# Tile 0 of x in two half loads on two queues, x 3 ahead of Q's second weight block, Q 0 and Q 1 in turn, and fewer idle matmuls, in a fused linear attention and SwiGLU kernel

## The chip, the cores and the metric

The kernel runs on one core of one Trainium2 chip. The metric is the device time of one execution in microseconds (us). The engines of the core are TensorE (PE in the profile, with its weight loads as PEld), VectorE (DVE), ScalarE (ACT), GpSimd (POOL) and SyncE (SP). Here only SP and ACT issue loads and stores; what they issue is shown as SPq and ACTq, and the transfers themselves are done by 16 DMA engines.

## The reference

The input x is 2048 rows of 512 bf16 numbers. The output is x plus two branches of the same layer-normed x.

```python
x = A_x                                             # (1, 2048, 512)
xn = (x - mean) / sqrt(var + 1e-5)                  # over the last axis
# branch A: linear attention, 32 heads of 16
q, k, v = split(xn @ wqkv)                          # wqkv (512, 1536)
phi = lambda t: where(t > 0, t + 1, exp(t)) + 1e-6
pq, pk = phi(q), phi(k)
num = pq @ (pk^T v) ; den = pq . sum_s(pk) + 1e-6   # per head
A = concat(num / den) @ wo
# branch B: SwiGLU, inner width 1792
B = (silu(xn @ w_gate) * (xn @ w_up)) @ w_down
return x + A + B
```

## The kernel before

The rows of x are cut into 16 tiles of 128 rows, held in `x_sb`. Tile t goes through mean and variance (`bns`, `agg`: DVE's bn_stats and bn_aggr), normalisation, a transpose, the projections to K and Q (four matmuls each, one for each block of 128 input columns: blocks 0 to 3 of the weights "wk" and "wq"), the feature map, and an accumulation (`gtacc`, L590) of xn^T times the K features. Only after all 16 tiles come the large products of the SwiGLU branch (L785) and the output products (L979, L990).

The first four tiles take a shorter way. They are only centred (`xc_half`, `xc_full`: x minus mean), transposed and projected, and the factor 1/std (`rstd`) is put in where ACT reads the result. For tiles 0 to 2 the transpose is done on TensorE (`tp_first`, L410, two matmuls against `ident` for each half) with a copy by ACT (`tc_first`, L422); for tile 3 it is a DMA transpose on SP's queue (`transpose_xc`, L401). The mean of tile 1 comes from ACT (`mean_act`, L307), not from DVE. `proj_part` (L465) is one projection matmul with one block; `proj_first` (L452) is two.

The order of the work is written out by hand. The program calls helpers in one list; each helper appends to the list of its engine, and each engine runs its list in order. Dependencies are kept by name: an operation waits for the last writer of each name it reads, and for the readers of each name it writes. Each DMA has its own semaphore. Two consequences matter here. The load of x 1 on ACT's queue reads the name ("ident",), so that it waits for POOL's memset of `ident`, and the affine_select (L242) that completes `ident` waits in turn for that load to land. And the transposes wait for `ident`.

Before x 0 is there, TensorE runs idle matmuls on constants: `fill(n, cols)` issues n matmuls of `cols` columns into bank 3 (L271). There are eight of 512 columns ahead of the first transpose, and one of 128 between the two halves of tile 0.

The loads are issued in this order. SP: x 0, K's blocks 0 and 1 in one load, K's block 2, x 2, Q's blocks 0 and 1, x 3, Q's blocks 2 and 3, x 4, x 5, x 6 with x 7. ACT: x 1, K's block 3. In K's projection TensorE takes the blocks in the order 0, 1, 3, 2; in Q's projection the order was blocks 0 and 1 of tile 1, blocks 0 and 1 of tile 0, the transposes of tile 2, and then blocks 2 and 3 in turn for the two tiles.

Of the kernel before, what the change touches and what calls it, by code (L numbers as in the profile page):

```python
# [10 lines left out]
P = 128  # L11
# [98 lines left out]
def bass_parallel_sum__linear_attn_block__swiglu_ffn__prompt_kernel(  # L110
# [10 lines left out]
    xin = A_x[0]  # L121
    oview = out[0]
    K = _Prog()
    pe, act, dve, pool, sp = nc.tensor, nc.scalar, nc.vector, nc.gpsimd, nc.sync
    bf, f32 = dt.bfloat16, dt.float32

    with contextlib.ExitStack() as es:
        E = es.enter_context

        def sb(name, shape, d=bf):  # L130
            return E(nc.sbuf_tensor(name, [P] + shape, d))

        x_sb = sb("x_sb", [NT, D])
# [14 lines left out]
        stats = sb("stats", [NT, 6], f32)  # L148
# [43 lines left out]
        def bk(i):  # L192
            return ("bank", i)
# [5 lines left out]
        def rows(v, t0, n):  # L199
            if t0 < NLONE:  # L200
                return v[t0 * P:(t0 + n) * P, :].rearrange("(t p) d -> p t d", p=P)
            return v[NLONE * P:, :].rearrange("(p t) d -> p t d", t=NT - NLONE)[:, t0 - NLONE:t0 - NLONE + n, :]

        def xload(eng, h, t0, n, after=()):
            K.dma(
                eng, lambda: h.dma_start(x_sb[:, t0:t0 + n, :], rows(xin, t0, n)),
                r=list(after), w=[("x", t0 + i) for i in range(n)],
            )

        def wqkv_load(eng, h, name, i, c0, n, after=()):  # L210
            K.dma(
                eng,
                lambda: h.dma_start(
                    wqkv_sb[:, c0:c0 + n, i * D:(i + 1) * D],
                    A_wqkv[c0 * P:(c0 + n) * P, i * D:(i + 1) * D].rearrange("(c p) f -> p c f", p=P),
                ),
                r=list(after), w=[(name, c) for c in range(c0, c0 + n)],
            )
# [6 lines left out]
        def whalf(name, dst, src, h):  # L225
# [6 lines left out]
                w=[(name, h)],  # L232
            )

        K.op("pool", lambda: pool.memset(warm[:, :], 0.0), w=[("warm",)])
        K.op("act", lambda: act.activation(warm[:, :], warm[:, :], ACT.Exp), r=[("warm",)], w=[("warm",)])

# [8 lines left out]
            r=[("ident",)], w=[("ident",)],  # L246
        )
        K.op("pool", lambda: pool.memset(nhalf[:, :], -0.5), w=[("nhalf",)])

        xload("sp", sp, 0, 1)  # L250
        wqkv_load("sp", sp, "wk", 1, 0, 2)
        wqkv_load("act", act, "wk", 1, 3, 1)
        wqkv_load("sp", sp, "wk", 1, 2, 1)
        xload("sp", sp, 2, 1)
        wqkv_load("sp", sp, "wq", 0, 0, 1)
        wqkv_load("sp", sp, "wq", 0, 1, 1)
        xload("sp", sp, 3, 1)
        wqkv_load("sp", sp, "wq", 0, 2, 1)
        wqkv_load("sp", sp, "wq", 0, 3, 1)
        xload("sp", sp, 4, 1)  # L260
# [6 lines left out]
        def fill(n, cols, after=()):  # L267
            K.op(
                "pe",
                [  # L270
                    (lambda: pe.matmul(banks[3][:, 0:cols], cw, cx[:, 0:cols], start=True, stop=True))  # L271
                    for _ in range(n)
                ],
                r=list(after), w=[bk(3)],
            )
# [20 lines left out]


        def bns(t):
            K.op("dve", lambda: dve.bn_stats(stats[:, t, :], x_sb[:, t, :]), r=[("x", t)], w=[("st", t)])  # L299

        def agg(t):
            K.op("dve", lambda: dve.bn_aggr(mv[:, t, :], stats[:, t, :]), r=[("st", t)], w=[("mv", t)])
# [95 lines left out]
        def transpose_xc(t):  # L398
            K.dma(
                "sp",  # L400
                lambda: sp.dma_start_transpose(out=xcT[:, NDC * t:NDC * (t + 1), :], in_=xc_sb[:, t, :]),  # L401
                r=[("xc", t, 0), ("xc", t, 1)], w=[("xcT", t, 0), ("xcT", t, 1)],
            )
# [57 lines left out]
        def proj_part(t, wname, c, pos):  # L461
            lo, b = (D, kb(t)) if wname == "wk" else (0, qb(t))
            K.op(
                "pe",
                lambda: pe.matmul(  # L465
                    banks[b], xcT[:, NDC * t + c, :], wqkv_sb[:, c, lo:lo + D],
                    start=(pos == 0), stop=(pos == NDC - 1),
                ),
                r=[("xcT", t, c // 2), (wname, c)], w=[bk(b)],
            )  # L470

        def kb(t):
            return 2 * (t % 2)

        def qb(t):
            return 2 * (t % 2) + 1
# [122 lines left out]
        def stat(t):  # L599
            bns(t)  # L600
            agg(t)
            eps(t, "pool")
            rstd_of(t)
# [3 lines left out]
            if t >= 3:  # L607
                transpose_dma(t)

        fill(8, 512)  # L610
        bns(0)
        agg(0)
        xc_half(0, 0)
# [10 lines left out]
        tp_first(1, 0, 6)  # L624
        tc_first(1, 0, 6)
        bns(1)
        rstd_of(0)
        xn_dve(0)
# [19 lines left out]
        proj_part(1, "wk", 3, 2)  # L648
        proj_part(1, "wk", 2, 3)
        proj_part(1, "wq", 0, 0)  # L650
        proj_part(1, "wq", 1, 1)
        transpose_xc(3)
        xload("sp", sp, 8, 2)
        xload("sp", sp, 10, 2)
        proj_part(0, "wq", 0, 0)
        proj_part(0, "wq", 1, 1)
        first_pk(0)
        tp_first(2, 0, 4)
# [429 lines left out]
```

## Time and profile before

| | |
|---|---|
| time, median of 3 runs | 210.25 us (210.12 to 210.37) |
| time of the profiled execution | 210.51 us |
| its span, first to last instruction | 209.3 us, so 1.2 us lie around it |
| TensorE busy | 206.6 us, 99% of the span |
| DVE, ACT, POOL busy | 120.2, 70.9, 72.0 us |
| DMA moved | 16.84 MB, mean 80 GB/s |

Rows of the timeline read: start in us, duration in us, engine, source line, operation, output tile <- input tiles, shape, count, and in brackets the idle time before it and what ended it. Where a count is over one, the duration runs from the start of the first to the end of the last. A matmul's duration includes its drain, so that matmuls in a row overlap; the spacing of their starts is what each costs. A row with an arrow from a tensor in DRAM and a number at its end is a load with its median time from issue to landing. Rows that begin with a stretch A:B give the length, the busy time of PE, PEld, DVE, ACT and POOL (with counts), the granted clock, the DMA share and GB/s.

### The profile page before, as it was taken

Reading aid. Unit: us, or ns where it says so; the run is one execution under the profiler, and the core shown is the slowest. Engines: PE = TensorE matmul, PEld = TensorE weight load, DVE = VectorE, ACT = ScalarE, POOL = GpSimd, SP = SyncE. Lnnn points to the kernel's source line nnn. Section 1 sums busy time; section 2 is a strip of 40 time slices with the busy share of each in tenths; the row PEclk is TensorE's granted clock in tenths of the full one; section 3 lists DMA queues with packets and bytes.
Section 4 is the critical chain, followed back from the end, with each engine's and each line's share of the span. In section 5 each row is a group of like instructions: output and inputs, shape, how many; then the busy total and the mean of one; then the engine's idle time right before and its main releaser. Section 6 shows DMA issues by size and latency. Waiting matters only on the chain.

```text
span 209.3 us, 2824 instructions
## 1 busy us (share of the span) xinstructions
PE 206.6 (99%) x1015; PEld 94.6 (45%) x1015; DVE 120.2 (57%) x246; ACT 70.9 (34%) x125; POOL 72.0 (34%) x90
## 2 busy tenths in 40 slices
PE   8999999999999999999999999999999999999996
PEld 3444444444444444444444444444444444444444
DVE  3999988336365874637355746365556545374122
ACT  5777666966643331312112312213031213121000
POOL 3427977568032543223041422240424132221200
PEclk9999999999999999999999999999999999999999
DMA  6673644894797011010101110102011010110101
GB/s 200 209 195 75 127 100 100 256 364 158 202 357 50 11 39 25 28 25 25 50 2 50 28 29 22 50 0 53 6 45 25 27 28 25 49 30 25 50 28 50
DMA packets 30287, 16.84 MB, mean 80 GB/s; under 512 B 20928, under 2 KB 29632, under 8 KB 30272
## 3 DMA queue, kind: packets, MB, share of 16 engines
q1 hardware_dynamic: 29984, 16.39, 29.9%
q10 hardware_dynamic: 288, 0.26, 0.4%
q8 instruction: 8, 0.13, 0.2%
q14 instruction: 7, 0.06, 0.1%
HBM read 9.70 MB, written 2.10 MB: 56 GB/s over the span
## 4 chain that ended last, share of the span: by engine, by line
PE 99%; DVE 0%; issue 0%
PE psum L785 46%; PE psum L990 23%; PE psum L438 10%; PE psum L979 7%; PE psum L590 7%; PE psum L271 2%; PE psum L465 2%; PE psum L452 2%; PE psum L410 1%; PE psum L892 0%; PE psum L915 0%; DVE out_sb L1003 0%
## 5 line engine op out<-in xcount | busy, mean ns | idle before, releaser
L800 ACT ACTIVATE sg<-psum 128x512 bf16<-128x512 f32 x56 | 33.4, 598 | 106.0 <-PE psum L785 102.5
L785 PE MATMUL psum<-xnT,wg_sb 128*128 128x512 bf16 x224 | 57.5, 379 | 0.0
L785 PE MATMUL psum<-xnT,wu_sb 128*128 128x512 bf16 x224 | 57.5, 379 | 0.0
L934 POOL TENSOR_TENSOR prod<-pkq,zb 128x512 f32<-128x512 bf16 x16 | 18.6, 1163 | 55.9 <-DVE pkq L514 55.9
L785 PEld LDWEIGHTS psum<-xnT,wu_sb 128*128 128x128 bf16 x224 | 21.9, 98 | 26.4
L785 PEld LDWEIGHTS psum<-xnT,wg_sb 128*128 128x128 bf16 x224 | 21.8, 98 | 26.2 <-issue 0.2
L1003 DVE TENSOR_TENSOR out_sb<-psum,x_sb 128x512 bf16<-128x512 f32 (+2 forms) x17 | 11.2, 660 | 35.9 <-PE psum L990 35.9
L958 POOL TENSOR_TENSOR pqn<-pkq,rden 128x512 bf16<-128x512 bf16 x16 | 16.9, 1056 | 36.5 <-DVE rden L952 36.5
L806 DVE TENSOR_TENSOR pkq<-psum,sg 128x512 bf16<-128x512 f32 x28 | 19.2, 686 | 17.1 <-PE psum L785 14.7
L806 DVE TENSOR_TENSOR xn_sb<-psum,sg 128x512 bf16<-128x512 f32 x28 | 18.8, 673 | 14.1 <-PE psum L785 13.6
L990 PE MATMUL psum<-wd_sb,xn_sb 128*128 128x512 bf16 (+2 forms) x126 | 25.7, 355 | 0.0
L990 PE MATMUL psum<-wd_sb,pkq 128*128 128x512 bf16 x112 | 25.5, 379 | 0.0
L438 PE MATMUL psum<-wqkv_sb,xnT 128*128 128x512 bf16 x96 | 22.5, 379 | 0.0
L582 POOL TENSOR_TENSOR zacc<-zacc,pkq 128x512 f32<-128x512 f32 x15 | 17.3, 1155 | 5.0 <-DVE ek L505 4.6
L990 PEld LDWEIGHTS psum<-wd_sb,xn_sb 128*128 128x128 bf16 x126 | 11.8, 98 | 12.5
L990 PEld LDWEIGHTS psum<-wd_sb,pkq 128*128 128x128 bf16 x112 | 11.0, 98 | 13.2
L979 PE MATMUL psum<-m_sb,eq 128*128 128x512 bf16 (+2 forms) x68 | 16.6, 366 | 0.0
L590 PE MATMUL psum<-pkq,xn_sb 128*128 128x512 bf16 x64 | 15.9, 379 | 0.0
L438 PEld LDWEIGHTS psum<-wqkv_sb,xnT 128*128 128x128 bf16 x96 | 9.4, 98 | 11.3
L942 DVE TENSOR_REDUCE den<-prod 128x32 f32<-128x512 f32 x16 | 10.9, 683 | 5.9 <-POOL prod L934 5.9
L299 DVE BATCH_NORM_STATS2 stats<-x_sb 128x6 f32<-128x512 bf16 x16 | 10.9, 681 | 3.4 <-DMA x_sb<-in_A_x_dram 3.4
L514 DVE SCALAR_TENSOR_TENSOR pkq<-pkq,eq 128x512 bf16<-128x512 bf16 x16 | 11.1, 692 | 0.6
(68 smaller groups left out, 138.7 us busy)
## 6 DMA issues: line engine op xcount, KB each, us to landing
out_dram<-out_sb SPq DMA_DIRECT2D x15, 128.0 KB, 1.7
wg_sb<-in_B_w_gate_dram SPq DMA_DIRECT2D x2, 896.0 KB, 7.8
wu_sb<-in_B_w_up_dram SPq DMA_DIRECT2D x2, 896.0 KB, 6.1
wd_sb<-in_B_w_down_dram SPq DMA_DIRECT2D x1, 1792.0 KB, 11.1
x_sb<-in_A_x_dram SPq DMA_DIRECT2D x5, 256.0 KB, 3.1
x_sb<-in_A_x_dram SPq DMA_DIRECT2D x5, 128.0 KB, 3.4
wqkv_sb<-in_A_wqkv_dram SPq DMA_DIRECT2D x5, 128.0 KB, 3.8
wqkv_sb<-in_A_wqkv_dram SPq DMA_DIRECT2D x1, 512.0 KB, 7.9
```

Of the source, the lines that this page charges most:

```text
L438: (lambda c=c: pe.matmul(banks[b], xnT[:, c, t * P:(t + 1) * P], wqkv_sb[:, c, lo:lo + D], start=(c == 0), stop=(c == NDC - 1),))
L514: lambda: dve.scalar_tensor_tensor(out=dst, in0=src, scalar=0.0, in1=e, op0=ALU.max, op1=ALU.add,),
L582: lambda: pool.tensor_tensor(out=zacc[:, :], in0=zacc[:, :], in1=pk, op=ALU.add),
L590: (lambda c=c: pe.matmul(banks[4 + c], xn_sb[:, t, c * P:(c + 1) * P], pkq[:, t, 0, :], start=(t == 0), stop=(t == NT - 1),))
L785: (lambda c=c: pe.matmul(banks[b], w_sb[:, c, fc * P:(fc + 1) * P], xnT[:, c, C * 512:(C + 1) * 512], start=(c == 0), stop=(c == NDC - 1),))
L800: lambda: act.activation(sg[:, j % NSG, :], banks[gb], ACT.Silu),
L806: lambda: dve.tensor_tensor(out=hT(C, fc), in0=banks[ub], in1=sg[:, j % NSG, :], op=ALU.mult,),
L934: lambda: pool.tensor_tensor(out=p, in0=pkq[:, t, 1, :], in1=zb[:, :], op=ALU.mult),
L958: lambda: pool.tensor_tensor(out=pqn[:, t % NPN, :].rearrange("p (i g h e) -> p g i h e", i=NB, g=NG, e=DH), in0=pkq[:, t, 1, :].rearrange ...
L979: (lambda g=g: pe.matmul(dst, pqnT(t)[:, g, :], m_sb[:, g, lo:hi], start=(g == 0), stop=False,))
L990: (lambda fc=fc: pe.matmul(dst, hT(C, fc)[:, jj * P:(jj + 1) * P], wd_sb[:, fc, lo:hi], start=False, stop=(fc == NFC - 1),))
L1003: lambda: dve.tensor_tensor(out=o, in0=src, in1=x_sb[:, t, lo:hi], op=ALU.add),
```

## The change

x 0 is loaded by two DMAs of 64 rows each, one as SP's first load and one as ACT's first load, ahead of all else on those engines. The second has a name of its own, ("xb", 0), and `bns` reads it too. On SP, x 3 is issued one place earlier, ahead of Q's block 1. The eight idle matmuls of 512 columns become seven of 512 and one of 128. In the list of projections, block 0 of Q is done for tile 1 and tile 0, then block 1 for tile 1 and tile 0; the issue of tile 3's DMA transpose and of two loads of x stands between them.

```diff
+        def xhalf(eng, h, t, lo, name):
+            K.dma(
+                eng, lambda: h.dma_start(x_sb[lo:lo + P // 2, t, :], rows(xin, t, 1)[lo:lo + P // 2, 0, :]),
+                w=[(name, t)],
+            )
+
+        xhalf("sp", sp, 0, 0, "x")
+        xhalf("act", act, 0, P // 2, "xb")
         K.op("pool", lambda: pool.memset(warm[:, :], 0.0), w=[("warm",)])
         K.op("act", lambda: act.activation(warm[:, :], warm[:, :], ACT.Exp), r=[("warm",)], w=[("warm",)])
...
-        xload("sp", sp, 0, 1)
         wqkv_load("sp", sp, "wk", 1, 0, 2)
         wqkv_load("act", act, "wk", 1, 3, 1)
         wqkv_load("sp", sp, "wk", 1, 2, 1)
         xload("sp", sp, 2, 1)
         wqkv_load("sp", sp, "wq", 0, 0, 1)
+        xload("sp", sp, 3, 1)
         wqkv_load("sp", sp, "wq", 0, 1, 1)
-        xload("sp", sp, 3, 1)
         wqkv_load("sp", sp, "wq", 0, 2, 1)
...
         def bns(t):
-            K.op("dve", lambda: dve.bn_stats(stats[:, t, :], x_sb[:, t, :]), r=[("x", t)], w=[("st", t)])
+            K.op("dve", lambda: dve.bn_stats(stats[:, t, :], x_sb[:, t, :]), r=[("x", t), ("xb", t)], w=[("st", t)])
...
-        fill(8, 512)
+        fill(7, 512)
+        fill(1, P)
         bns(0)
...
         proj_part(1, "wq", 0, 0)
-        proj_part(1, "wq", 1, 1)
+        proj_part(0, "wq", 0, 0)
         transpose_xc(3)
         xload("sp", sp, 8, 2)
         xload("sp", sp, 10, 2)
-        proj_part(0, "wq", 0, 0)
+        proj_part(1, "wq", 1, 1)
         proj_part(0, "wq", 1, 1)
```

## The prediction

> **What bounds the kernel now.** I read the page first (busy shares, slices, chain), then the chain of waits in order of time, then the timeline of the first 12 us, then the landings of single loads.
>
> ```profile
> PE 206.6 (99%) x1015; PEld 94.6 (45%) x1015; DVE 120.2 (57%) x246; ACT 70.9 (34%) x125; POOL 72.0 (34%) x90
> PE   8999999999999999999999999999999999999996
> PE 99%; DVE 0%; issue 0%
> ...
> 0.84 3.57 PE psum L271 x8
> 4.41 0.36 PE psum L410 x2
> ```
>
> TensorE is busy for 99% of the span and is the chain from 0.84 us to the end. Nothing the diff touches lies later than the first 12 us, so the question is only how much earlier or later TensorE's stream leaves its opening. The opening starts with eight idle matmuls (L271) and goes on with the transposes of tile 0 (L410). The busy row hides two holes there, because a matmul's shown duration covers its drain; the weight loads (PEld) show them.
>
> ```profile
> 2.93 0.15 PEld L271 LDWEIGHTS psum<-const-bfloat16-1.0 128*128 128x128 bf16 x1 [0.28 <-issue]
> 3.35 0.15 PEld L271 LDWEIGHTS psum<-const-bfloat16-1.0 128*128 128x128 bf16 x1 [0.28 <-issue]
> 3.08 0.69 DVE L299 BATCH_NORM_STATS2 stats<-x_sb 128x6 f32<-128x512 bf16 x1 [3.08 <-DMA x_sb<-in_A_x_dram]
> 3.81 0.18 DVE L302 BATCH_NORM_AGGREGATE mv<-stats 128x2 f32<-128x6 f32 x1
> 4.03 0.48 DVE L382 TENSOR_SCALAR xc_sb<-x_sb,mv 128x256 bf16<-128x256 bf16 x2
> 4.37 0.13 PEld L410 LDWEIGHTS psum<-ident,xc_sb 128*128 128x128 bf16 x2 [0.87 <-DVE xc_sb L382]
> ```
>
> Idle matmuls follow each other every 0.42 us (2.93, 3.35). The last loads at 3.35 + 0.42 = 3.77 and has streamed by about 4.2; the first transpose starts at 4.37, released by DVE's centred tile, which goes back to tile 0's landing (bn_stats at 3.08). So the bound of the opening is not the idle matmuls but the chain x 0, statistics, centring; the idle matmuls end 0.17 ahead of it.
>
> ```profile
> 5.31 0.66 PE L465 MATMUL psum<-wqkv_sb,xcT 128*128 128x512 bf16 x2
> 5.91 0.10 PEld L465 LDWEIGHTS psum<-wqkv_sb,xcT 128*128 128x128 bf16 x1 [0.45 <-ACT xcT L422]
> 4.80 1.25 ACT L422 ACTIVATE xcT<-psum 128x256 bf16<-128x256 bf16 x4 [0.71 <-PE psum L410]
> 8.32 1.03 PE L465 MATMUL psum<-wqkv_sb,xcT 128*128 128x512 bf16 x4
> ```
>
> Second hole: K's first two blocks for tile 0 start at 5.31 and 5.31 + 0.66 - 0.38 = 5.59, the third, block 3, has its weights loaded only at 5.91. The page names ACT's copy, but of the four copies from 4.80 to 6.05 the second, which is the one needed, had ended near 5.5. The other input of that matmul is K's block 3 of weights, loaded on ACT's queue.
>
> ```profile
> 1.48 0.45 ACTq L213 DMA_DIRECT2D wqkv_sb<-in_A_wqkv_dram  x1
> wqkv_sb<-in_A_wqkv_dram ACTq DMA_DIRECT2D x1, 128.0 KB, 4.3
> ```
>
> Issued at 1.48 and 4.3 us to landing: 5.78, which is what the weight load at 5.91 waited for. The four matmuls of the row at 8.32 (1.03 for four, 0.38 each with its drain) give a spacing of (1.03 - 0.38) / 3 = 0.217 at full clock against 0.42 at the start. Between 5.31 and 5.59 lies a mixture: 0.28 = part at 0.42, rest at 0.217, which puts the change of clock near 5.44. After 5.91 TensorE runs at 0.217 without a hole.
>
> **The loads.** ACT gets a new first load.
>
> ```profile
> 0.80 0.39 SPq L206 DMA_DIRECT2D x_sb<-in_A_x_dram  x1
> 0.80 1.28 ACT L236 ACT_TABLE_LOAD   x1 [0.80 <-PEq L1073]
> 1.07 0.38 ACTq L206 DMA_DIRECT2D x_sb<-in_A_x_dram  x1
> 1.25 0.93 SPq L213 DMA_DIRECT2D wqkv_sb<-in_A_wqkv_dram  x2
> 3.37 0.63 ACT L307 ACTIVATE scr<-x_sb 128x512 bf16<-128x512 bf16 x1 [1.08 <-DMA x_sb<-in_A_x_dram]
> 1.80:2.20 0.40, 0.40 (x3) 0.13 (x1) 0.00 (x0) 0.39 (x2) 0.00 (x0) 1.00 0.47 151
> 2.20:2.70 0.50, 0.50 (x3) 0.17 (x2) 0.00 (x0) 0.09 (x1) 0.00 (x0) 1.00 1.07 373
> ```
>
> From issue to first use x 0 takes 3.08 - 0.80 = 2.28 us on SP and x 1 takes 3.37 - 1.07 = 2.30 on ACT. In the first 0.4 us of traffic only SP's rows flow, at 151 GB/s (last number); with both queues in flight it is 373. If one queue's rate is what limits x 0, its first 60 KB (0.4 x 151) came in that stretch and the other 68 KB shared 373 with x 1, done about 68 / 187 = 0.36 later, at 2.56; two queues at twice 151 would have brought all 128 KB by about 2.22. So the split is worth between 0.34 us and nothing, or minus 0.05 for a second semaphore that bn_stats now waits for and ACT's own 0.02 of delay. I take the middle, 0.17. Here the Trainium skill (DMA: Bandwidth & Descriptors, Rules for kernel authors) speaks against the change: two transfers to disjoint partition halves spray over the same 16 engines, so one 128-partition transfer is advised. By it the gain is zero; the 151 against 373 in this trace says that the engines are not yet full when x 0 arrives, and there the two differ.
>
> With 0.17: transposes start at 4.37 - 0.17 = 4.20. The idle matmuls, 384 columns shorter (0.75 x 0.42 = 0.32), stop near 3.89 instead of 4.2. That cut alone gains nothing: 0.17 was idle already, and what waits is DVE's chain. If x 0 gains nothing, TensorE simply idles 0.48 instead of 0.17. What it avoids is that an idle matmul runs past 4.20.
>
> The price stands on ACT's queue. The table load ran beside the x 1 load (0.80 for 1.28, and 1.07), so it does not hold the issue; but xb at 0.80 takes a slot, and loads on a queue follow each other at 0.41 (ACT, 1.07 to 1.48) to 0.45 (SP, 0.80 to 1.25). So x 1 is issued at about 1.25 and K's block 3 at 1.66, each 0.18 later.
>
> ```profile
> 3.57 0.29 POOL L242 TENSOR_SCALAR_AFFINE_SELECT ident<-ident 128x128 bf16<-128x128 bf16 x1 [2.54 <-DMA x_sb<-in_A_x_dram]
> 3.91 0.19 ACT L307 ACTIVATION_READ_ACCUMULATOR scr<-x_sb 128x1 f32 x1
> 4.42 0.48 DVE L382 TENSOR_SCALAR xc_sb<-x_sb,mact 128x256 bf16<-128x256 bf16 x2
> 4.67 0.85 PE L410 MATMUL psum<-ident,xc_sb 128*128 128x128 bf16 x6
> ```
>
> x 1 later by 0.18 reaches two things. POOL's identity waits for x 1's landing: it ends at 3.86, then 4.04, still ahead of 4.20. ACT's mean of tile 1 ends at 4.10, then 4.28; DVE's centring of tile 1 started at 4.42 behind tile 0's, and could now start at 4.33, its first half done (0.28) at 4.61. The transposes of tile 1 are the third pair of six plus two, at 4.20 + 0.5 = 4.7. So 0.18 is covered, with about 0.1 to spare; beyond that it counts one for one.
>
> Then K's first matmul starts at 5.31 - 0.17 = 5.14. It is at half clock until 5.44 (0.30 of 0.42, 0.71 done), the rest takes 0.06: the second at 5.50, not 5.59, and the third could start at 5.72. Of the 0.17 the clock keeps half. And there the third block's landing decides: with the same 4.3 us it is 1.66 + 4.3 = 5.96, weight load at 6.09, plus 0.18 against now. The bytes ahead of it are the same as before, so by the other reading it lands at 5.78 as now, and the change is 0. Only a landing below 5.6 would let the 0.1 to 0.2 through. So the sum in the profiled execution is 0 to +0.18, with -0.22 (5.72 against 5.94) as its best end.
>
> ```profile
> 7.24 0.59 PE L465 MATMUL psum<-wqkv_sb,xcT 128*128 128x512 bf16 x2
> 7.45 0.10 PEld L465 LDWEIGHTS psum<-wqkv_sb,xcT 128*128 128x128 bf16 x1
> 2.70 0.91 SPq L213 DMA_DIRECT2D wqkv_sb<-in_A_wqkv_dram  x2
> 3.64 0.43 SPq L206 DMA_DIRECT2D x_sb<-in_A_x_dram  x1
> wqkv_sb<-in_A_wqkv_dram SPq DMA_DIRECT2D x1, 128.0 KB, 3.8
> x_sb<-in_A_x_dram SPq DMA_DIRECT2D x1, 128.0 KB, 3.7
> 7.58 0.69 DVE L299 BATCH_NORM_STATS2 stats<-x_sb 128x6 f32<-128x512 bf16 x1
> 11.64 0.23 PEld L452 LDWEIGHTS psum<-wqkv_sb,xcT 128*128 128x128 bf16 x2 [0.20 <-ACT kpos L528]
> ```
>
> The swap on SP: Q's block 1 (the second of the two from 2.70, issued 3.17, 3.8 to landing, 6.97) takes x 3's place (3.64 + 3.7 = 7.34) and x 3 takes its. Of the two Q matmuls from 7.24 the second, at 7.45, takes block 1, and a weight load stands one matmul ahead of its own, so block 1 was needed at 7.24; in turn with Q 0 it is needed one matmul later, at 7.45. So 0.1 remains where 0.27 was: no wait and no gain, if TensorE comes no earlier than now. x 3 at 6.97 helps nobody: DVE took it at 7.58 without idling, behind tile 2. Tile 3's transposed copy, needed at 11.64, therefore comes when it came. The order of the Q matmuls costs nothing; the same sixteen go through at 0.217.
>
> **The profiled execution and the median.** It took 210.51 us, span 209.3 and 1.2 around it; the median of the three runs is 210.25. Sums are made as differences in the profiled execution and put on the median: 210.25 + 0 to 0.18, in the lower half because some executions will have an earlier block 3: 210.3. About 0.2% (0.42 us) is what a measurement of this kernel can tell from no change, so faster means under 209.83 and slower over 210.67.
>
> **Rivals.**
> (1) Faster: everything in the opening gives way. The idle cut is 0.32, the hole before the transposes 0.17, the hole before block 3 is 5.94 - 5.80 = 0.14, in all 0.63, of which the half clock until 5.44 takes back about 0.15: 210.25 - 0.48 = 209.77. For it: 151 against 373 GB/s, and that block 3's 4.3 us is long beside x 1's 2.3 and may be a slow landing of this execution. Against it: x 0 would have to land 0.34 earlier, and the identity would be ready at 4.04 at the earliest. 0.17.
> (2) Slower: ACT's third load. Between ACT's first load (2.3 us) and its second (4.3) lie 2 us for a place in the queue. Now x 1 holds the second place and block 3 the third. If a quarter of the 2 us falls on x 1, it lands 0.18 + 0.5 late, the identity ends at 4.54 and the first transpose waits for it to 4.6; block 3 comes 0.5 late as well, to 6.4 for 5.91. The two overlap: +0.5 to +0.6, 210.8. It decides from the point where block 3 lands after 6.2, or x 1 is used after 3.8. 0.23.
> (3) Slower by the clock: the hole ahead of the transposes grows from 0.17 to 0.3 to 0.5. From the first matmul to full clock it took 5.44 - 0.84 = 4.6 us. If that count starts again at 4.20, full clock comes at 8.8, 3.36 us later; 3.36 us at 0.42 are 8 matmuls that take 1.73 at 0.217: +1.6, 211.9. Against it: the clock came in spite of the first hole. 0.08. The Trainium skill (TensorE: Matmul & The Clock Gate, Part 1) has the clock decided by free-running windows of about 3.4 us, so that one window missed would cost about 1.7, an estimate from that page; no row here shows a window.
> That the split does nothing at all for x 0 gives 0 to +0.18 too, because block 3 decides then as well; it is part of the forecast.
>
> **The numbers.** Forecast (no change, 210.3, own range 210.0 to 210.65) 0.52; faster 0.17; slower by the queue 0.23, by the clock 0.08. Faster 0.17, same 0.52, slower 0.31. The range runs from rival 1 to a little over rival 2, 209.75 to 210.9, and leaves out the clock and the outer parts of both.
>
> **What the changed profile would show.** Right: x 0's bn_stats near 2.9, the first transpose near 4.2, K's block 3 again later than the matmul before it, loaded at 5.8 to 6.1, from there no hole. Wrong: bn_stats at 3.08 or later (split worth nothing); block 3 not waited for and the stream after it over 0.2 ahead (rival 1); POOL's identity or ACT's mean as what the transposes wait for, or block 3 after 6.2 (rival 2); matmuls 0.42 apart well past 5.5 (rival 3); a wait at Q's block 1 (the swap's cover was too short).

## The result and the profile after

The changed kernel takes 211.52 us (median of 9 runs, 210.65 to 212.74) against 210.25 before (210.07 to 210.68): ratio 1.0075, 95% interval 1.0053 to 1.0096. It is slower, and its times are spread over 2.1 us where the old ones lie within 0.6. (The ratio is that of the two whole sets of times, not of their medians; where the times are spread I give median and extremes too.) The profiled execution after is the fastest of the nine, 210.65 us, and already shows half of the cause. First its loads and what waits for x 0, from the timeline, with the two stretches of traffic that the prediction used:

```profile
0.80 0.58 SPq L237 DMA_DIRECT2D x_sb<-in_A_x_dram  x1
0.80 0.56 ACTq L237 DMA_DIRECT2D x_sb<-in_A_x_dram  x1
1.44 0.83 SPq L213 DMA_DIRECT2D wqkv_sb<-in_A_wqkv_dram  x1
1.47 0.53 ACTq L206 DMA_DIRECT2D x_sb<-in_A_x_dram  x1
1.80:2.20 0.40, 0.40 (x3) 0.12 (x1) 0.00 (x0) 0.40 (x1) 0.00 (x0) 1.00 0.09 18
2.20:2.70 0.50, 0.50 (x3) 0.17 (x2) 0.00 (x0) 0.49 (x2) 0.00 (x0) 1.00 1.03 230
3.43 0.69 DVE L306 BATCH_NORM_STATS2 stats<-x_sb 128x6 f32<-128x512 bf16 x1 [3.43 <-DMA x_sb<-in_A_x_dram]
3.94 0.29 POOL L250 TENSOR_SCALAR_AFFINE_SELECT ident<-ident 128x128 bf16<-128x128 bf16 x1 [2.91 <-DMA x_sb<-in_A_x_dram]
4.72 0.39 PE L417 MATMUL psum<-ident,xc_sb 128*128 128x128 bf16 x2 [0.63 <-DVE xc_sb L389]
5.59 2.75 PE L472 MATMUL psum<-wqkv_sb,xcT 128*128 128x512 bf16 x12
```

A load of 64 rows takes 0.58 us to issue, longer than the 0.39 of the whole tile. Between 1.80 and 2.20 us 18 GB/s arrive, not 151, and in the stretch behind it 230, not 373. bn_stats starts at 3.43 for 3.08, the first transpose at 4.72 for 4.37. The idle matmuls have streamed by about 3.89, so TensorE stands still for 0.83 us (a hole, counted from the end of the last idle matmul's streaming, without its drain, to the first transpose; the bracket of the row counts from the end of the drain). The chain now shows the wait for x 0 as a load:

```profile
0.80 2.60 DMA x_sb<-in_A_x_dram
...
3.43 0.70 DVE stats L306
```

In this execution full clock came before 5.2 and the twelve projections went through in 2.75. They end at 5.59 + 2.75 = 8.34, where before's, from 5.31 in 2.96, ended at 8.27, so almost all was caught up. A second profile of the same kernel, 213.11 us, shows the other executions:

```profile
1.43 1.08 SPq L213 DMA_DIRECT2D wqkv_sb<-in_A_wqkv_dram  x2
1.48 0.79 ACTq L206 DMA_DIRECT2D x_sb<-in_A_x_dram  x1
x_sb<-in_A_x_dram ACTq DMA_DIRECT2D x1, 128.0 KB, 3.6
5.26 0.29 POOL L250 TENSOR_SCALAR_AFFINE_SELECT ident<-ident 128x128 bf16<-128x128 bf16 x1 [4.23 <-DMA x_sb<-in_A_x_dram]
5.70 0.37 PE L417 MATMUL psum<-ident,xc_sb 128*128 128x128 bf16 x2 [1.61 <-POOL nhalf L256]
6.62 4.24 PE L472 MATMUL psum<-wqkv_sb,xcT 128*128 128x512 bf16 x12
```

x 1 is issued at 1.48 behind xb, 0.05 after SP's load of K's blocks 0 and 1, needs 0.79 to issue and some 3.6 to land, near 5.0. The identity waits for it, the first transpose starts at 5.70 (named after the memset behind the identity on POOL), and then the twelve projections take 4.24 for 2.75: the first eight start 0.42 apart, which is half clock, and the rest 0.22 apart.

### The profile page after: what moved, and what is told of

It reads as the page before. It is cut to its first block, busy times and chain, and to the rows that moved or that the text cites. A ratio compares the mean times of both kernels' runs of the same rounds, so it can differ in the third digit from the quotient of the medians.

```text
span 209.4 us, 2826 instructions
## 1 busy us (share of the span) xinstructions
PE 206.1 (98%) x1015; PEld 94.3 (45%) x1015; DVE 120.0 (57%) x246; ACT 70.9 (34%) x125; POOL 72.1 (34%) x90
## 4 chain that ended last, share of the span: by engine, by line
PE 97%; DMA 1%; DVE 1%; issue 0%
PE psum L793 46%; PE psum L998 23%; PE psum L445 10%; PE psum L987 7%; PE psum L597 7%; PE psum L472 2%; PE psum L459 2%; DMA x_sb<-in_A_x_dram 1%; PE psum L417 0%; DVE stats L306 0%; PE psum L900 0%; PE psum L923 0%; DVE xc_sb L389 0%; DVE out_sb L1011 0%; DVE mv L309 0%
```

## The experiments

**The parts alone.** e1: only the idle matmuls, `fill(8, 512)` to `fill(7, 512)` and `fill(1, P)`.

> The kernel before with only the idle matmuls cut (seven of 512 columns and one of 128). Theory (hole and clock): TensorE idles about 0.48 us ahead of the first transpose instead of 0.17, x 0 lands as before; in some executions full clock is granted later, so the median is 0.1 to 0.8 us above before and the spread of the times grows beyond 1 us. Rival (loads): only the loads matter, and they are as before: median within 0.15 us of before, spread as before (about 0.6 us).

Ratio 1.0008 (0.9998 to 1.0018), 210.26 to 210.97. No loss that can be measured; here the theory expected too much. In its profile the transposes start at 4.27, so a hole of 0.38 us cost nothing:

```profile
4.27 0.39 PE L410 MATMUL psum<-ident,xc_sb 128*128 128x128 bf16 x2 [0.18 <-DVE xc_sb L382]
5.52 2.04 PEld L465 LDWEIGHTS psum<-wqkv_sb,xcT 128*128 128x128 bf16 x10 [0.17 <-ACT xcT L422]
```

e2: only the two half loads, with `bns` reading ("xb", 0).

> The kernel before with only x 0 in two half loads on two queues. Theory: both half loads are issued in about 0.57 us instead of 0.39, x 0 is used about 0.35 us later than before (3.43 for 3.08), and a hole of about 0.5 us stands ahead of the first transpose; full clock comes later in some executions: median 0.3 to 0.9 us above before, wider spread. Rival (loads alone): the whole loss of the change is here, plus 1.0 to 1.3 us, with a spread as after.

Median 212.78 (210.75 to 213.49), ratio 1.0095 (1.0066 to 1.0123): the whole loss. Its median lies above the change's, but the intervals of the two ratios overlap. Its profile, 211.61, pairs with the one of 213.11 above; the two kernels differ only in the parts that e1 and e3 found free. x 1 is late here too, and the transposes start at 5.82, but behind the hole the clock is full:

```profile
x_sb<-in_A_x_dram ACTq DMA_DIRECT2D x1, 128.0 KB, 3.7
5.82 0.27 PE L417 MATMUL psum<-ident,xc_sb 128*128 128x128 bf16 x2 [1.41 <-POOL nhalf L256]
6.60 2.75 PE L472 MATMUL psum<-wqkv_sb,xcT 128*128 128x512 bf16 x12
```

The twelve projections differ by 4.24 - 2.75 = 1.49, the two executions by 213.11 - 211.61 = 1.50. So two costs come on top of each other: a late x 1, and half clock.

e3: only x 3 ahead of Q's block 1 and the Q matmuls in turn.

> The kernel before with only x 3 ahead of Q's block 1 and the Q matmuls in turn. Theory: nothing moves, within 0.15 us of before, no wait at Q's block 1. Rival (order): the loss of the change is in the swap, plus 0.5 us or more.

Ratio 1.0011 (0.9999 to 1.0022). Nothing, as expected.

e12: the changed kernel with x 0 in one load again (e1 and e3 together).

> The changed kernel with x 0 in one load again: the idle matmuls cut, x 3 ahead and Q in turn. Theory (the split is all of it): within 0.25 us of before. Rival (the parts add up only together): 0.5 us or more above before.

Ratio 1.0010 (1.0000 to 1.0020), 210.25 to 210.81; the median, 210.69, is 0.36 above before's beside it, a little over the 0.25 that I allowed, and the ratio only just tells it from nothing. So the split is nearly all of the loss; what is left is 0.2 us by the ratio and 0.4 by the medians. In its profiled execution (210.73) TensorE waited once for a block of Q, block 3, whose load the swap does not move:

```profile
8.96 0.60 PE L465 MATMUL psum<-wqkv_sb,xcT 128*128 128x512 bf16 x2 [0.39 <-DMA wqkv_sb<-in_A_wqkv_dram]
```

**Late load or half clock.** e4: the changed kernel with `fill(8, 512)` and `fill(5, P)`, so that TensorE is busy until the first transpose if x 1 is in time.

> The changed kernel with idle matmuls until about 4.74 us (eight of 512 columns and five of 128), so that TensorE has no hole ahead of the first transpose, which still starts near 4.72. Theory (hole and clock): the loss goes but for the later transposes, median 0 to 0.4 us above before and a spread under 0.8 us. Rival (loads alone): as after, 1.0 to 1.3 us above before.

Median 211.47; eight of ten at 210.88 to 211.62, two at 213.1 and 213.56. The theory missed: the median is 1.12 above before, as the rival had it. Times over 212.3 are two of ten here and four of nine in the changed kernel, too few to call it a smaller tail. x 1 was taken for harmless here; with x 1 late there can be a hole again behind the longer fill. Its profile (x 1 in time, transposes at 4.62) is the fastest run, and it shows that x 1's winning has a price too:

```profile
wqkv_sb<-in_A_wqkv_dram SPq DMA_DIRECT2D x1, 256.0 KB, 4.3
5.88 2.75 PE L472 MATMUL psum<-wqkv_sb,xcT 128*128 128x512 bf16 x12 [0.39 <-ACT xcT L429]
```

K's blocks 0 and 1, issued at 1.44, take 4.3 to land for 2.9 before the change, so near 5.7, and the first projection starts only at 5.88, 1.26 behind the first transpose (0.94 before). The row names ACT's copy, but the copy that it needs was the first of four from 4.94, 0.3 each.

Two more profiles: e5, the changed kernel again (shown above), and e6, e2's kernel again.

> The changed kernel once more, for a second profile. Theory (race): x 1 on ACT and K's blocks 0 and 1 on SP are issued within 0.05 us of each other near 1.45 us; the queue that comes second in the race gets its issue stretched to about 0.8 us and its data over 1 us later. Where x 1 loses it lands near 5.2, the identity waits for it and the first transpose starts near 5.8 (time 211.5 or more); where it wins it lands near 3.7 and the time is about 210.7. Rival (clock): x 1 lands at 3.7 in slow executions too, and matmuls stay 0.42 us apart past 5.5.

> The kernel with only the half loads once more, for a second profile. As for the changed kernel: race says that a time over 211.3 goes with x 1 landing after 5 us and a first transpose near 5.8; clock says that it goes with half clock past 5.5 us; over 212.5 may need both.

e5 took 213.11, e6 214.11. Both have the late x 1 (landed near 5.0 and 5.95) and half clock: race and clock together, not one of them. Of the profiles with xb ahead of x 1 at 0.80 and K's 256 rows on SP, x 1 landed near 3.7 in two (after, e4; issued at 1.47) and at 5.0 to 6.0 in four (e2, e5, e6, e10; issued at 1.48).

e10: the changed kernel with `fill(12, 512)`.

> The changed kernel with twelve idle matmuls of 512 columns, so that TensorE has no hole before about 5.9 us and every execution starts its transposes there at the earliest. Theory (late x 1 plus a window at half clock because of the hole): every execution pays the later start, about 1.1 to 1.3 us, but no half clock after it, so 211.3 to 211.8 with a spread under 0.8 us and nothing over 212.3. Rival (loads alone): the slow executions stay at 212.4 to 213.5.

211.41 to 211.83, median 211.56, in five executions: as the theory said. The late start alone costs 1.2 (before beside it: 210.33), and with no hole nothing is over 212.

e15 and e16: the kernel before with `fill(6, 512)` and `fill(4, 512)`; the loads are untouched.

> The kernel before with six idle matmuls of 512 columns for eight: hole ahead of the first transpose about 1.0 us, loads as before, first transpose still near 4.3. Clock theory (a hole of 1.2 us or more lets a stretch of 3.4 us at half clock follow in some executions, 0.5 to 0.8 us do not): at the edge, median within 0.5 us of before, at most a third of the executions 1.2 us or more above. Rival (only late loads cost): within 0.15 us of before, no times over 211.3.

> The same with four idle matmuls: hole about 1.9 us. Clock theory: in half or more of the executions 1.2 to 1.9 us above before (211.5 to 212.2), with matmuls 0.42 us apart far past 5.5 us in such a profile and no transpose later than before. Rival (only late loads cost): within 0.15 us of before.

e15: three executions at 210.08 to 210.24, eight at 211.71 to 212.84. e16: 211.13 to 212.73, median 211.93, all eight above before's longest (211.02). The projections before, and then the profile of e15 (211.71):

```profile
5.31 2.96 PE L465 MATMUL psum<-wqkv_sb,xcT 128*128 128x512 bf16 x12
```

```profile
0.84 2.72 PE L271 MATMUL psum<-const-bfloat16-1.0 128*128 128x512 bf16 x6 [0.84 <-PEq L1073]
4.27 0.40 PE L410 MATMUL psum<-ident,xc_sb 128*128 128x128 bf16 x2 [0.71 <-DVE xc_sb L382]
5.20 4.27 PE L465 MATMUL psum<-wqkv_sb,xcT 128*128 128x512 bf16 x12
```

The transposes start at 4.27, no later than before, and the same twelve projections take 4.27 where before's took 2.96. Nothing but the idle matmuls differs, so a hole (here 0.92 us, 3.35 to 4.27) is enough by itself for half clock behind it; going by the times it was in eight of eleven executions, where I had expected a third at most. But the hole's length does not decide it alone: behind e2's hole of 1.6 us (4.20 to 5.82) the clock was full.

**What makes x 1 late.** e7: both half loads on SP, ACT's queue as before.

> The kernel before with x 0 in two half loads, both on SP's queue one behind the other; ACT's queue as before. Race theory: no two loads are issued at the same moment, x 1 lands near 3.4, x 0 near 3.3 (one place of 0.45 later, less rows); median 0.1 to 0.4 us above before, nothing over 211.5. Rival (splitting): half loads as such are the harm: about 1 us or more above before, with times over 212.5.

212.49 to 213.34, ratio 1.0126 (1.0110 to 1.0141). My theory fell and the rival's numbers came true: no two loads of x 0 are issued at the same moment, and it is worse than the change.

```profile
0.80 1.21 SPq L252 DMA_DIRECT2D x_sb<-in_A_x_dram  x2
1.07 0.38 ACTq L206 DMA_DIRECT2D x_sb<-in_A_x_dram  x1
4.12 0.69 DVE L306 BATCH_NORM_STATS2 stats<-x_sb 128x6 f32<-128x512 bf16 x1 [4.12 <-DMA x_sb<-in_A_x_dram]
5.41 0.40 PE L417 MATMUL psum<-ident,xc_sb 128*128 128x128 bf16 x2 [1.00 <-DVE xc_sb L389]
```

The 64 rows alone take 0.58 each to issue (1.21 for two), x 0 is used only at 4.12, and a hole of 1.2 us follows. The long first issue belongs to the load of 64 rows, not to two queues at once.

e8: halves on two queues, ACT's held back to 1.07 by the identity's memset.

> The kernel before with x 0 in two half loads on two queues, but ACT's half waits for the identity's memset as x 1's load did, so that it is issued near 1.07 and not beside SP's at 0.80. Race theory: issues take 0.4 us each again, x 0 lands near 3.2 to 3.3, x 1 is issued near 1.48, clear of SP's 1.25, and lands between 3.8 and 4.5: median 0.2 to 0.8 us above before, and no times over 212.3. Rival (place in the queue): x 1 behind another load on ACT is late however it is issued: over 1 us above before.

Median 212.84 (211.41 to 213.61). The race theory, which allowed nothing over 212.3, fell again, and the rival (place in the queue) held: x 1 is issued at 1.64, 0.2 behind SP's, and lands near 5.44.

```profile
0.81 1.28 ACT L243 ACT_TABLE_LOAD   x1 [0.81 <-PEq L1080]
1.64 0.64 ACTq L206 DMA_DIRECT2D x_sb<-in_A_x_dram  x1
```

This settles one more rival: in the changed kernel ACT's table load starts only behind xb's issue, near 1.40, just before x 1's; here it starts at 0.81, as before the change, and x 1 is late all the same. The stretches of this run show the clock most plainly (the last three numbers are granted clock, DMA share, GB/s; execution of 213.61):

```profile
3.80:7.15 3.35, 1.36 (x13) 0.64 (x11) 1.81 (x7) 1.41 (x5) 1.12 (x4) 1.00 1.03 337
7.20:10.60 3.40, 3.40 (x10) 1.27 (x9) 3.29 (x12) 1.74 (x4) 1.49 (x3) 0.50 0.57 182
10.65:14.00 3.35, 3.35 (x20) 1.59 (x18) 2.37 (x8) 2.39 (x6) 2.61 (x5) 1.00 0.51 95
```

Full clock was already granted at 3.80. In that stretch TensorE was busy for 1.36 of 3.35 us; the next 3.4 us were granted 0.50, though TensorE was busy throughout; then 1.00 again. The Trainium skill (TensorE: Matmul & The Clock Gate, Part 1) has free-running windows of 3413 ns decide the next stretch; this trace agrees, with steps of 3.4. When the first step to full clock comes differs from one execution to the next: near 3.6 in e9's profile, 3.8 here, 5.4 before the change. That may be why the same kernel pays in some executions and not in others; no run shows it.

e9: before, with x 1's load on ACT issued at once beside x 0's, 128 rows each.

> The kernel before with x 1's load on ACT issued at once, beside x 0's on SP, each of 128 rows; the identity then no longer waits for x 1. Theory A (64 rows are the cost): both loads take about 0.4 us to issue, x 0 is used at 3.1 to 3.2 and x 1 before 3.4; no hole beyond before's, within 0.3 us of before, no times over 211.3. Theory B (two queues at the same moment are the cost): both take about 0.57 us, x 0 is used at 3.4, K's loads behind race, 0.5 us or more above before.

210.48 to 211.19, ratio 1.0015 (1.0004 to 1.0025). Issues 0.41 and 0.40: 128 rows at the same moment are not stretched.

```profile
1.80:2.20 0.40, 0.40 (x3) 0.12 (x1) 0.00 (x0) 0.40 (x1) 0.00 (x0) 1.00 0.73 59
3.61 0.69 DVE L299 BATCH_NORM_STATS2 stats<-x_sb 128x6 f32<-128x512 bf16 x1 [3.61 <-DMA x_sb<-in_A_x_dram]
3.65 0.38 PE L271 MATMUL psum<-const-bfloat16-1.0 128*128 128x512 bf16 x1
4.90 0.28 PE L410 MATMUL psum<-ident,xc_sb 128*128 128x128 bf16 x2 [0.87 <-DVE xc_sb L382]
```

But x 0 was used at 3.61 all the same, 0.5 later than before the change. What slowed it is not shown: up to 2.20 only SP's rows flowed here too, at 59 GB/s for 151. The hole was 1.0 us (the last idle matmul, at 3.65, runs at full clock and has streamed by 3.87; the transposes start at 4.90). That is longer than e15's 0.92, yet none of the eleven executions has the tail. In this profile full clock had come ahead of the hole; in e8's it had too, but there the hole was 2.2 (4.0 to 6.16) and half clock followed.

e11: the changed kernel with x 1 as SP's second load, the identity no longer waiting for it.

> The changed kernel with x 1's load as SP's second load, ahead of K's blocks 0 and 1, and not behind xb on ACT; the identity no longer waits for it. Theory (x 1 loses to the 256-row load of K that stands 0.05 us ahead of it): x 1 lands at 3.5 to 4.2, first transpose at 4.5 to 4.8, no times over 212, median 0.2 to 0.9 us above before. Rival (place does not matter): as after, with a part of the executions over 212.3.

210.94 to 211.17, ratio 1.0034 (1.0021 to 1.0048). With x 1 in time none of five executions has the tail. What is left is the late x 0 (transposes at 4.68) and K's blocks 0 and 1, now SP's third load, for which the first projection waits:

```profile
1.44 0.56 SPq L206 DMA_DIRECT2D x_sb<-in_A_x_dram  x1
1.48 0.79 ACTq L213 DMA_DIRECT2D wqkv_sb<-in_A_wqkv_dram  x1
4.68 0.28 PE L417 MATMUL psum<-ident,xc_sb 128*128 128x128 bf16 x2 [0.59 <-DVE xc_sb L389]
5.80 2.84 PE L472 MATMUL psum<-wqkv_sb,xcT 128*128 128x512 bf16 x12 [0.25 <-DMA wqkv_sb<-in_A_wqkv_dram]
```

The load on ACT takes 0.79 to issue though it is now one of weights: the place is slow, not x 1.

e13: x 0 in two halves by columns (all 128 rows, 256 columns each), else as the change.

> The changed kernel with the two loads of x 0 cut by columns (all 128 rows, 256 columns each) and not by rows. If 64 rows are the cost: each issues in about 0.4 us, K's load follows on SP near 1.25 and x 1 on ACT near 1.25 to 1.3, x 1 lands at 3.5 to 4, median at most 0.6 above before, nothing over 212. If any load ahead of x 1 on ACT is the cost: x 1 lands near 5 in a part of the executions, 1 us or more above before at the median, times over 212.3.

Median 212.61 (211.31 to 213.22). Its profile (212.77):

```profile
0.80 0.40 ACTq L237 DMA_DIRECT2D x_sb<-in_A_x_dram  x1
0.80 0.40 SPq L237 DMA_DIRECT2D x_sb<-in_A_x_dram  x1
1.29 0.38 ACTq L206 DMA_DIRECT2D x_sb<-in_A_x_dram  x1
x_sb<-in_A_x_dram ACTq DMA_DIRECT2D x1, 128.0 KB, 3.0
1.80:2.20 0.40, 0.40 (x3) 0.13 (x1) 0.00 (x0) 0.40 (x1) 0.00 (x0) 1.00 0.48 147
3.08 0.69 DVE L306 BATCH_NORM_STATS2 stats<-x_sb 128x6 f32<-128x512 bf16 x1 [3.08 <-DMA x_sb<-in_A_x_dram]
4.96 0.37 PE L417 MATMUL psum<-ident,xc_sb 128*128 128x128 bf16 x2 [0.87 <-POOL nhalf L256]
```

Here the issues are short, x 0 is used at 3.08 as before the change, and x 1 still lands at 4.3, and half clock follows. So the tail does not need the 64 rows. In all the kernels with a load ahead of x 1 on ACT (the change, e8, e13) x 1 is issued 0.03 to 0.2 behind SP's load of K's 256 rows, where before the change it went out 0.18 ahead of it.

e14: the changed kernel with SP's second load cut to K's block 0 alone.

> The changed kernel with SP's second load cut to K's block 0 alone (128 rows for 256); block 1 goes with block 2. If x 1 waits out the load that wins against it: half of the lateness goes, x 1 lands at 4.2 to 4.6 where it loses, first transpose near 5.0 to 5.2, nothing over 212.3, median 0.4 to 0.9 above before. If the size of that load does not matter: as after, x 1 near 5.1 where it loses, times over 212.3.

Its profile (211.02):

```profile
1.48 0.79 ACTq L206 DMA_DIRECT2D x_sb<-in_A_x_dram  x1
x_sb<-in_A_x_dram ACTq DMA_DIRECT2D x1, 128.0 KB, 3.1
5.21 0.27 PE L417 MATMUL psum<-ident,xc_sb 128*128 128x128 bf16 x2 [1.16 <-POOL nhalf L256]
```

x 1 lands near 4.55 instead of 5.0 to 6.0 and the first transpose starts at 5.21: about half of the lateness went with half of that load, in this one profile. Six executions took 210.91 to 211.43, but four 212.72 to 213.42, so the tail that I had excluded stayed. Behind the profiled hole of 1.3 us the clock was full; what the four had is not shown.

## Why the prediction was wrong

The forecast was no change, 210.3 with a range to 210.9; 211.52 is outside. The late x 1 and the half clock stood in the rivals, but were sized too small and kept apart; that x 0 could come 0.35 later than before was in none of them.

The step that failed first is "I take the middle, 0.17" for x 0. The rate of 151 against 373 GB/s was read as room that a second queue fills. With two loads issued at the same moment the stretch from 1.80 to 2.20 brought 18 GB/s (after), 59 (e9) and 147 (e13), never twice 151. With the issue at its old length (e13) the split is worth nothing (3.08), and with 64 rows it costs 0.35 in the profile after. Of that 0.19 is the issue: "a slot" of 0.39 for a half tile was taken over from a whole one and measures 0.58. The rest is not explained. The 0.05 for a second semaphore is seen in no run; e13 waits for two and starts at 3.08. The Trainium skill's rule against splitting by partitions (DMA: Bandwidth & Descriptors, Rules for kernel authors) was weighed and set aside; the runs side with it, and go further: a loss, not only no gain.

The second, and the largest, is "So 0.18 is covered" for x 1. The landing was assumed to move with the issue, and the issue by 0.18. The issue moved by 0.40 (1.07 to 1.47), since a slot is longer. The use of x 1 by ACT moved by 0.37 in the better profiled execution of the change and by 1.7 (3.37 to 5.07) in the other. That x 1 then waits out SP's load of K's 256 rows is read from its place (e11) and from that load's size (e14); what the two loads do to each other in the engines is not seen. Rival 2 named this wait, the identity and its place, but priced x 1 at 0.7 late and put the harm at 0.5 to 0.6. The late start alone is 1.2 (e10).

The third is the clock at 0.08 as a case of its own. Its price, +1.6, was right: 1.49 between the two paired executions. But its hole was put at "0.3 to 0.5", and it follows from the late loads: 0.83 and 1.8 were measured. Rivals 2 and 3 are one chain of events, and the range that ended at rival 2 left their sum out. e1 shows that a hole of 0.38, as I had sized it, is harmless.

Right were: the idle cut alone gains nothing (e1); the swap on SP and the order of Q cost nothing (e3); and that the identity and ACT's mean would be what the transposes wait for in the bad case.

Wrong too was that block 3's weights decide. In the profile after, twelve projections from 5.59 take 2.75, which is (2.75 - 0.38) / 11 = 0.215 each: no hole at the third. With the start late, block 3 is there in time. Nor does e1, with the loads and the start of before, wait at the third (its weight loads run from 5.52 without a gap): the hole belonged to the one execution that I had read.

Open stays which of two loads wins in one execution; that 64 rows take longer to issue was seen in every run, not explained; when a hole brings half clock, beyond that it can; and for the executions without a profile the split into late x 1 and half clock is only read from the groups of their times. One thing was not run: the changed kernel with only the identity freed from waiting for x 1's load. That wait comes from the program's names, and without it tile 0 might start in spite of a late x 1.

## What to carry to other kernels

Before a load is put ahead of another on a queue, ask what big load on the other queue the displaced one will then meet, and take its price from what it meets, not from its old time to landing. Idle matmuls ahead of a wait are an insurance: they cost nothing while the wait is the bound, and here 0.9 us without them lost 1.3 us or more in most executions (e15), while 0.4 us lost nothing (e1). Cut them only against the latest landing, not the one in the profile, and price a late landing and the half clock behind it together.

## What the runs showed of the hardware

As a queue's first load a DMA of 64 rows of 1 KB took 0.53 to 0.58 us to issue and one of 128 rows 0.38 to 0.41, whether the other queue's first load was issued at the same moment (after, e9) or 0.27 later (e7, before). A stretch of 3.4 us in which TensorE was busy for 1.36 was followed by 3.4 us at a granted clock of 0.50, even where full clock had been reached before it (e8). e1, e11 and e9, with holes of 0.38, 0.79 and 1.03 us in their profiles, had no execution over 211.2; e15, with 0.92, had eight of eleven over 211.7. So these runs give no one length of hole above which the clock falls.
